# Dealing the opening loads of a transformer kernel over two DMA queues in the order of need

## The chip, the cores and the metric

The kernel runs on 1 core of one Trainium2 chip. The metric is device time in microseconds (us), lower is better. The six runs of the kernel before lie within 0.7 us of each other. "Faster" or "slower" needs 2%. Engines: TensorE (PE, with its weight loads PEld), VectorE (DVE), ScalarE (ACT), GpSimd (POOL), SyncE (SP). "SPq" and "ACTq" are DMA issues by SyncE's and ScalarE's sequencers. A load has "landed" when its semaphore tells that all its data are there.

## The reference, cut to what matters

Two rounds of a windowed attention layer and a gated MLP, on 2048 tokens of width 1024, bf16. Only the first steps of the first layer matter here: layer norm of x, then q = norm(x) times the first 1024 columns of `wqkv`.

```python
x = A_x                                                  # 1 x 2048 x 1024
x = x + _A_ref(_layernorm(x), A_wqkv, A_wo)              # qkv = norm(x) @ wqkv, attention, @ wo
x = x + _B_ref(_layernorm(x), B_w1, B_w3, B_w2)          # (silu(xn @ w1) * (xn @ w3)) @ w2
x = x + _A_ref(_layernorm(x), A_wqkv, A_wo)
x = x + _B_ref(_layernorm(x), B_w1, B_w3, B_w2)
```

## The kernel before

The kernel lists its operations with estimated durations, places them in a small model of the engines, and emits them in the order of the modelled start. Each engine then works through its own list in that fixed order. The queue "AQ" is a model: in the model it is an engine of its own, but its loads are issued by ScalarE and stand in ScalarE's list, between its activations.

```python
def dma(kb, dst, src, reads, writes, cls=3, transpose=False, queue="SP"):
    def emit(op):
        if queue == "AQ":
            nc.scalar.dma_start(dst, src)      # ScalarE's own instruction list
        ...
        else:
            nc.sync.dma_start(dst, src)
    return pr.add(queue, 0.45, emit, reads, writes, cls, size=kb * 1024)
```

PE starts with ten warm-up matmuls on a constant (line 285), while the first loads are under way. The opening works on four blocks of 128 tokens, x0 to x3, and on the q weights, cut into eight "rows" of 128 x 1024 (256 KB each). x0 comes as two halves. Blocks 0 and 1 are multiplied without waiting for their variance: half of x0's sum is formed on VectorE, the other half on ScalarE, the mean is subtracted, PE transposes the result, and the weight matmuls of blocks 0 and 1 start, row by row. Blocks 2 and 3 are normalized meanwhile and multiplied afterwards.

```python
def q_first():
    for hh in range(2):                                   # x0: one half on each queue
        dma(128, x_sb[0][:, hh * 512:(hh + 1) * 512], ..., queue="AQ" if hh else "SP")
    dma(256, x_sb[1][:], xin[:, 1, :], ..., queue="AQ")
    rows = q_weights(0, "k", load=False)
    for kk in range(4):
        rows[2](kk)                                       # rows 0 to 3, SyncE
    load_x(0, 2, 4)                                       # x2, x3, SyncE
    rows[2](4)
    rows[2](5)
    ...
    act(0.75, ... accum_out=part[:, 1:2] ...)             # ScalarE: sum of x0's second half
    rows[2](6, 2, queue="AQ", after=[("part", 1)])        # rows 6 and 7, one load, ScalarE
    ...                                                   # mean, subtract, transposes
    for j in range(2, TPC):
        stats(j)                                          # VectorE: statistics of x2, x3
        ...
    # PE (line 509): rows 0 to 2 for x0, rows 0 to 2 for x1, then rows 3 to 7 for both
    for kk, j0, j1 in [(k, j, j + 1) for j in range(2) for k in range(3)] + [(k, 0, 2) for k in range(3, KT)]:
        ...
    # PE (line 523): all rows for x2 and x3
```

Of the kernel before, what the change touches and what calls it, by code (L numbers as in the profile page):

```python
# [156 lines left out]
def kernel(  # L157
# [42 lines left out]
    def alloc(name, shape, dt=BF16):  # L200
        return sb.tile(shape, dt, name=name)
# [31 lines left out]
    part = alloc("part", [P, 2], FP32)  # L233
# [14 lines left out]
    def dve(dur, emit, reads, writes, cls=2, **kw):  # L248
        return pr.add("DVE", dur, emit, reads, writes, cls, **kw)

    def act(dur, emit, reads, writes, cls=0, **kw):
        return pr.add("ACT", dur, emit, reads, writes, cls, **kw)
# [4 lines that stand above are left out]
                nc.scalar.dma_start(dst, src)  # L257
            elif transpose:
                nc.sync.dma_start_transpose(dst, src)
# [3 lines that stand above are left out]
# [34 lines left out]
    def load_x(c, j0=0, j1=TPC, after=()):  # L297
        for j in range(j0, j1):
            n = c * TPC + j
            dma(256, x_sb[n][:], xin[:, n, :], after, [("x", n, 0), ("x", n, 1)], 0 if c == 0 else 3)  # L300
# [3 lines left out]
    def ln(c, first=False):  # L304
        s = stage_no[0]
        b, q = s % 2, s % 4
        xb = xnT[b]

        def stats(j, after=()):
            n = c * TPC + j  # L310
            pri = -9 if first else 1
            for hh in range(2):
                dve(0.67, lambda _, hh=hh: nc.vector.bn_stats(st[q][:, j, hh, :],  # L313
                                                              x_sb[n][:, hh * 512:(hh + 1) * 512]),
                    [("x", n, hh)] + list(after), [("st", q, j, hh)], pri)
            dve(0.2, lambda _: nc.vector.bn_aggr(mv[q][:, j, :], st[q][:, j, :, :]),  # L316
                [("st", q, j, 0), ("st", q, j, 1)], [("mv", q, j)], pri)

        def root(j0, j1):
            act(0.3, lambda _: nc.scalar.activation(sd[q][:, j0:j1], mv[q][:, j0:j1, 1], ACTF.Sqrt, bias=epst[:]),  # L320
                [("mv", q, j) for j in range(j0, j1)] + ["eps"], [("sd", q, j) for j in range(j0, j1)], -9 if first else 0, table="sqrt")
            dve(0.16, lambda _: nc.vector.reciprocal(rstd[q][:, j0:j1], sd[q][:, j0:j1]),
                [("sd", q, j) for j in range(j0, j1)], [("rstd", q, j) for j in range(j0, j1)], -9 if first else 0)

        def apply(j):
            n = c * TPC + j
            dve(0.5, lambda _: nc.vector.tensor_scalar(xn[j][:], x_sb[n][:], mv[q][:, j, 0:1], rstd[q][:, j:j + 1],  # L327
                                                       op0=ALU.subtract, op1=ALU.mult),
                [("x", n, 0), ("x", n, 1), ("mv", q, j), ("rstd", q, j)], [("xn", j)] + [("xn", j, h) for h in range(2)], -9 if first else 1)

        if first:
            return b, q, stats, root, apply
        for j in range(TPC):
            stats(j)
        root(0, TPC)
        for j in range(TPC):
            apply(j)
            dma(256, xb[:, :, j * P:(j + 1) * P], xn[j][:], [("xn", j)],
                [("xnT", b, j)] + [("xnT", b, j, h) for h in range(2)], 0, transpose=True)
        return b  # L340
# [17 lines left out]
    def q_weights(which, split, load=True, after=()):  # L358
        ids = [take_slot(), take_slot()]
        if not load:  # L360
            def row(kk, n=1, after=(), **kw):
                i = ids[kk // 4]
                v = slot[i][:].rearrange("p (k c) -> p k c", k=4)
                dma(256 * n, v[:, kk % 4:kk % 4 + n, :], wqkv_v[:, kk:kk + n, which * D:(which + 1) * D], after,
                    [("w", i, kk % 4 + z) for z in range(n)], 0, **kw)
            return ids, split, row
        for h, i in enumerate(ids):
            if split != "c":
                v = slot[i][:].rearrange("p (k c) -> p k c", k=4)
                dma(1024, v, wqkv_v[:, 4 * h:4 * h + 4, which * D:(which + 1) * D], after,  # L370
                    [("w", i, k) for k in range(4)], 3)
            else:
                v = slot[i][:].rearrange("p (k c) -> p k c", k=KT)
                dma(1024, v, wqkv_v[:, :, which * D + h * 512:which * D + (h + 1) * 512], [],
                    [("w", i, k) for k in range(4)], 3)
        return ids, split
# [43 lines left out]
    def transposed(src, keys, dst, dkeys):  # L420
        for h, add, fn, dur in ((0, dve, nc.vector.tensor_copy, 0.42), (1, act, nc.scalar.copy, 0.59)):
            a = Acc()
            k0 = 4 * h

            def tr(op, a=a, k0=k0):
                pt = bank[a.bank][:].bitcast(BF16)
                for k in range(4):
                    nc.tensor.transpose(pt[:, k * P:(k + 1) * P], src[:, (k0 + k) * P:(k0 + k + 1) * P], ident[:])  # L428
            tro = pr.add("PE", 0.25, tr, [keys[h], "ident"], [], takes=[a], lag=0.17, lane=2)

            def emit(op, a=a, k0=k0, fn=fn):
                pt = bank[a.bank][:].bitcast(BF16)
                fn(dst[:, k0:k0 + 4, :], pt[:, 0:4 * P].rearrange("p (k t) -> p k t", k=4))
            evac(add, dur, emit, tro, [], dkeys[k0:k0 + 4], a, cls=-9)

    def q_first():
        for hh in range(2):
            dma(128, x_sb[0][:, hh * 512:(hh + 1) * 512], xin[:, 0, hh * 512:(hh + 1) * 512], [], [("x", 0, hh)], 0,
                queue="AQ" if hh else "SP")
        dma(256, x_sb[1][:], xin[:, 1, :], [], [("x", 1, 0), ("x", 1, 1)], 0, queue="AQ")  # L440
        rows = q_weights(0, "k", load=False)
        wslots[0] = rows[:2]
        for kk in range(4):
            rows[2](kk)
        load_x(0, 2, 4)
        rows[2](4)
        rows[2](5)
        b, q, stats, root, apply = ln(0, first=True)
        ce = hT[:, 8:16, :]
        dve(0.45, lambda _: nc.vector.tensor_scalar(xn[2][:, 0:512], x_sb[0][:, 0:512], 0.0, 0.0, op0=ALU.add,  # L450
# [1 line left out]
            [("x", 0, 0)], [("xn", 2), ("part", 0)], -9)  # L452
        act(0.75, lambda _: nc.scalar.activation(xn[3][:, 0:512], x_sb[0][:, 512:1024], ACTF.Copy,
                                                 accum_out=part[:, 1:2]), [("x", 0, 1)], [("xn", 3), ("part", 1)], -9)
        rows[2](6, 2, queue="AQ", after=[("part", 1)])
        dve(0.16, lambda _: nc.vector.tensor_scalar(mean[:, 0:1], part[:, 0:1], part[:, 1:2], 1.0 / D, op0=ALU.add,
                                                    op1=ALU.mult), [("part", 0), ("part", 1)], [("mean", 0)], -9)
        act(1.15, lambda _: nc.scalar.activation(xn[3][:], x_sb[1][:], ACTF.Copy, scale=1.0 / D,
# [7 lines left out]
            transposed(xn[j], [("xn", j, h) for h in range(2)], ce[:, :, j * P:(j + 1) * P],  # L466
                       [("ce", j, k) for k in range(KT)])
        for j in range(2, TPC):
            stats(j)
            root(j, j + 1)  # L470
            apply(j)
            transposed(xn[j], [("xn", j)] * 2, xnT[b][:, :, j * P:(j + 1) * P],
                       [("xnT", b, j, k // 4) for k in range(KT)])
# [233 lines left out]
    def attend(l, c):  # L707
        for r in range(R):
            t_stage(l, c * R + r)

    q_first()
    attend(0, 0)
    for c in range(1, NCH):
# [47 lines left out]
```

## Time and profile before

| | before |
|---|---|
| median of 6 runs | 1616.09 us (1615.54 to 1616.23) |
| profiled span | 1614.2 us |
| PE busy | 1601.5 us |
| first weight matmul (line 509) | 5.89 us |
| idle of PE at row 4 | 0.91 us, from 10.25 to 11.16 |
| second half of the opening (line 523) starts | 15.56 us |

The page of the kernel before; first its busy times, then the chain that ended last, by engine.

```profile
PE 1601.5 (99%) x7463; PEld 762.6 (47%) x7610; DVE 1121.5 (69%) x1904; ACT 331.3 (21%) x527; POOL 5.2 (0%) x28
...
PE 99%; DMA 1%; issue 0%; SPq 0%; DVE 0%
```

PE is the bound nearly everywhere. The waits of PE over the whole span (who waited for what: us in total, times, longest):

```profile
PE bank L509 <- DMA slot<-in_A_wqkv_dram: 0.9, 1, 0.9
PE bank L285 <- PEq L745: 0.8, 1, 0.8
PE bank L509 <- DVE hT L433: 0.3, 1, 0.3
```

These three waits are all that the view lists, and all lie in the opening: a change of the loads can win about 0.9 us. (The trace of this kernel lacks 147 matmul records, 7463 against 7610 weight loads, so PE's busy time is understated.) The timeline of PE (start, length, what) shows where. Matmuls are pipelined, so lengths overlap a little.

```profile
4.98 0.66 PE L428 MATMUL bank<-ident,xn 128*128 128x128 bf16 x8
5.89 1.05 PE L509 MATMUL bank<-hT,slot 128*128 128x128 bf16 x16 [0.25 <-DVE hT L433]
...
7.42 2.83 PE L509 MATMUL bank<-hT,slot 128*128 128x128 bf16 x40
11.16 2.79 PE L509 MATMUL bank<-hT,slot 128*128 128x256 bf16 x24 [0.91 <-DMA slot<-in_A_wqkv_dram]
...
15.56 7.15 PE L523 MATMUL bank<-xnT,slot 128*128 128x256 bf16 x64
```

ScalarE in the same time. Its issue of rows 6 and 7 (ACTq at 3.57) stands behind the first activation on x0 (line 453).

```profile
0.80 0.88 ACTq L257 DMA_DIRECT2D x<-in_A_x_dram  x2
2.02 0.20 ACT L281 ACTIVATE preload<-const-float32-0.0 128x1 f32<-128x1 f32 x1
3.56 0.63 ACT L453 ACTIVATE xn<-x 128x512 bf16<-128x512 bf16 x1 [1.34 <-DMA x<-in_A_x_dram]
3.57 0.39 ACTq L257 DMA_DIRECT2D slot<-in_A_wqkv_dram  x1
```

### The profile page before, as it was taken

The numbers are of one execution on the slowest core, as the hardware profiler recorded it, in microseconds if no ns is written. First come the engines' busy times: TensorE is split into PE (matmuls) and PEld (weight loads), VectorE is DVE, ScalarE is ACT, GpSimd is POOL, SyncE is SP. The second block draws the span as 40 slices with busy tenths as digits, with TensorE's granted clock in tenths as the row PEclk, the third lists the DMA queues.
The fourth block names the chain that finished last, engine by engine and source line by source line (L and its number), as shares of the span: only waits on it lengthen the run. The fifth ranks groups of instructions, "written<-read, shape, count | busy, mean of one in ns | idle before, by whom it ended". The sixth has DMA issues, their size and how long they took to land.

```text
span 1614.2 us, 19079 instructions
## 1 busy us (share of the span) xinstructions
PE 1601.5 (99%) x7463; PEld 762.6 (47%) x7610; DVE 1121.5 (69%) x1904; ACT 331.3 (21%) x527; POOL 5.2 (0%) x28
## 2 busy tenths in 40 slices
PE   9999999999999999999999999999999999999999
PEld 6555544444444444444444444444444444444444
DVE  5898888889889888888898729884288832211211
ACT  5423322021211222113211032110321101101110
POOL 1000000000000000000000000000000000000000
PEclk9999999999999999999999999999999999999999
DMA  9834755395548664758645487365873464454451
GB/s 320 228 100 150 224 170 171 118 225 168 171 136 251 195 190 132 217 167 234 189 136 160 160 243 231 122 173 176 253 221 119 158 181 156 144 176 150 156 165 44
DMA packets 350777, 285.80 MB, mean 177 GB/s; under 512 B 72288, under 2 KB 344928, under 8 KB 350688
## 3 DMA queue, kind: packets, MB, share of 16 engines
q1 hardware_dynamic: 350128, 283.67, 58.2%
q8 instruction: 59, 0.97, 0.2%
q10 hardware_dynamic: 560, 0.92, 0.2%
q14 instruction: 30, 0.25, 0.0%
HBM read 238.94 MB, written 29.36 MB: 166 GB/s over the span
## 4 chain that ended last, share of the span: by engine, by line
PE 99%; DMA 1%; issue 0%; SPq 0%; DVE 0%
PE bank L347 98%; DMA slot<-in_A_wqkv_dram 1%; PE bank L523 0%; PE bank L509 0%; PE bank L428 0%; SPq L261 0%; DVE x L688 0%
## 5 line engine op out<-in xcount | busy, mean ns | idle before, releaser
L347 PE MATMUL bank<-xnT,slot 128*128 128x512 bf16 x4955 | 1088.9, 379 | 5.3
L347 PEld LDWEIGHTS <-slot 128*128 128x128 bf16 x5056 | 518.1, 102 | 573.0
L347 PE MATMUL bank<-slot,hT 128*128 128x512 bf16 (+2 forms) x1812 | 387.3, 372 | 1.9
L658 DVE TENSOR_TENSOR hT<-sg,bank 128x512 bf16<-128x512 bf16 x224 | 153.4, 685 | 213.0 <-PE bank L347 196.3
L265 DVE TENSOR_TENSOR scr<-scr 128x1024 bf16<-128x1024 bf16 (+3 forms) x576 | 292.1, 535 | 2.1
L347 PEld LDWEIGHTS <-hT 128*128 128x128 bf16 x1848 | 178.5, 98 | 208.7
L656 ACT ACTIVATE sg<-bank 128x512 bf16<-128x512 f32 x224 | 133.8, 597 | 653.8 <-PE bank L347 613.6
L265 DVE TENSOR_TENSOR scr<-qT,kT 128x2048 bf16<-128x2048 bf16 x128 | 153.7, 1216 | 71.7 <-DMA kT<-qkv_d 70.1
L405 ACT CAST sgt<-bank 128x512 bf16<-128x512 f32 x184 | 107.9, 586 | 290.9 <-PE bank L347 273.1
L265 DVE TENSOR_TENSOR scr<-pA,vT 128x2048 bf16<-128x2048 bf16 x128 | 152.5, 1216 | 0.4
L688 DVE TENSOR_TENSOR x<-x,bank 128x512 bf16<-128x512 bf16 (+1 forms) x66 | 43.7, 669 | 122.7 <-PE bank L347 122.4
L347 PE MATMUL bank<-wo,oT 128*128 128x512 bf16 x502 | 112.6, 379 | 0.5
L313 DVE BATCH_NORM_STATS2 st<-x 128x6 f32<-128x512 bf16 x124 | 81.5, 679 | 11.5 <-DMA x<-in_A_x_dram 11.0
L347 PEld LDWEIGHTS <-oT 128*128 128x128 bf16 x512 | 50.1, 98 | 60.3
L633 DVE TENSOR_TENSOR x<-x,bank 128x512 bf16<-128x512 bf16 x64 | 43.9, 685 | 36.5 <-PE bank L347 35.0
L320 ACT ACTIVATE sd<-mv,epst 128x4 f32<-128x4 f32 (+1 forms) x17 | 5.1, 299 | 182.4 <-DVE mv L316 181.9
L616 DVE STREAM_TRANSPOSE pA<-pB 128x2048 bf16<-128x2048 bf16 x16 | 37.0, 2310 | 0.4
L593 DVE STREAM_TRANSPOSE pB<-pA 128x2048 bf16<-128x2048 bf16 x16 | 37.0, 2310 | 0.4
L656 ACT ACT_TABLE_LOAD x20 | 25.7, 1283 | 51.3 <-PE bank L347 51.1
L265 DVE TENSOR_TENSOR pA<-scr 128x256 bf16<-128x256 bf16 x128 | 35.3, 282 | 0.3
L327 DVE TENSOR_SCALAR xn<-x,mv,rstd 128x1024 bf16<-128x1024 bf16 x62 | 30.8, 541 | 4.6 <-DMA xnT<-xn 4.5
L265 DVE TENSOR_TENSOR oT<-scr 128x256 bf16<-128x256 bf16 x128 | 33.6, 282 | 0.1
(60 smaller groups left out, 210.0 us busy)
## 6 DMA issues: line engine op xcount, KB each, us to landing
slot<-in_B_w_dram SPq DMA_DIRECT2D x160, 1024.0 KB, 5.8
slot<-in_A_wqkv_dram SPq DMA_DIRECT2D x28, 1024.0 KB, 5.2
qkv_d<-sgt SPq DMA_DIRECT2D x92, 256.0 KB, 3.4
qT<-qkv_d SPq DMA_DIRECT2D x16, 512.0 KB, 5.0
slot<-in_B_w_dram SPq DMA_DIRECT2D x16, 512.0 KB, 5.5
kT<-qkv_d SPq DMA_DIRECT2D x14, 544.0 KB, 6.6
vT<-qkv_d SPq DMA_DIRECT2D x14, 544.0 KB, 5.7
out_dram<-x SPq DMA_DIRECT2D x31, 128.0 KB, 4.2
```

Source lines behind the costliest of these rows:

```text
L265: return lambda _: nc.vector.tensor_tensor(o, a, b, op=op)
L313: dve(0.67, lambda _, hh=hh: nc.vector.bn_stats(st[q][:, j, hh, :], x_sb[n][:, hh * 512:(hh + 1) * 512]), [("x", n, hh)] + list(after), [( ...
L320: act(0.3, lambda _: nc.scalar.activation(sd[q][:, j0:j1], mv[q][:, j0:j1, 1], ACTF.Sqrt, bias=epst[:]), [("mv", q, j) for j in range(j0, ...
L327: dve(0.5, lambda _: nc.vector.tensor_scalar(xn[j][:], x_sb[n][:], mv[q][:, j, 0:1], rstd[q][:, j:j + 1], op0=ALU.subtract, op1=ALU.mult), ...
L347: nc.tensor.matmul(bank[a.bank][:, 0:ncol], lhsT=w, rhs=r, start=first and i == 0, stop=last and i == n - 1)
L405: evac(act, 0.59, lambda _, a=a, i=i, m=m: nc.scalar.copy(sgt[i][:, m % 2, :], bank[a.bank][:]), op, [], [("sgt", i, m % 2)], a)
L593: dve(2.31, lambda _: nc.vector.transpose(psmT[:].rearrange("p c d -> p (c d)"), psm[:].rearrange("p w s -> p (w s)")), allA, ["pB"])
L616: dve(2.31, lambda _: nc.vector.transpose(At[:].rearrange("p w s -> p (w s)"), AeT[:].rearrange("p c d -> p (c d)")), ["pB"], allA)
L633: evac(dve, t1(512), lambda _, xs=xs, a=a: nc.vector.tensor_tensor(xs, xs, bank[a.bank][:], op=ALU.add), op, [("x", n, hh)], [("x", n, hh) ...
L656: evac(act, 0.6, lambda _, i=i, a=ag: nc.scalar.activation(sg[i][:], bank[a.bank][:], ACTF.Silu), og, [], [("sg", i)], ag, table="silu")
L658: evac(dve, t1(512), lambda _, i=i, a=au, f=f: nc.vector.tensor_tensor(hT[:, f, :], sg[i][:], bank[a.bank][:], op=ALU.mult), ou, [("sg", i ...
L688: evac(dve, t1(cn), lambda _, xs=xs, a=a, cn=cn: nc.vector.tensor_tensor(xs, xs, bank[a.bank][:, 0:cn], op=ALU.add), op, [("x", n, hh)], [ ...
```

## The change: its intent, and the diff

The intent is to give each row of weights a place in the order of need, by dealing the loads over both queues. Rows 2, 3 and 4 move to ScalarE's queue; x2 and x3 go ahead of rows 5 to 7 on SyncE's. Since x2 can now come early, its statistics are held until the copy of x1's transpose, so that they don't get in VectorE's way.

```diff
-        for kk in range(4):
+        for kk in range(2):
             rows[2](kk)
+        for kk in range(2, 5):
+            rows[2](kk, queue="AQ")
         load_x(0, 2, 4)
-        rows[2](4)
         rows[2](5)
+        rows[2](6, 2)
 ...
-        rows[2](6, 2, queue="AQ", after=[("part", 1)])
 ...
         for j in range(2, TPC):
-            stats(j)
+            stats(j, [("ce", 1, 0)])
```

## The prediction

> **What bounds the kernel.** TensorE (PE). The page gives PE 1601.5 us of a 1614.2 us span, and the chain that ended last is 99% PE, 1% DMA. The waits of PE from 25 us to the end list nothing. The change touches only the first 15 us, so its ceiling is PE's idle time there. The timeline of PE shows it: nothing before 0.77 (launch), 0.25 us before the first weight matmuls at 5.89 (a VectorE copy), and 0.91 us from 10.25 to 11.16, put down to a load of the q weights. That last gap is what can be won: 0.06% of the time.
>
> **Why the gap is there.** By the trace SyncE issues x0's half, weight rows 0 to 3, then x2 (3.08), x3 (4.98), row 4 (5.71), row 5 (6.08). x3 and row 4 are held until rows 0 and 1 have landed (4.97, 5.70): loads reuse a few completion semaphores, and the ninth and later wait for an early one. ScalarE's queue brings x0's other half, x1 (landed 5.15), and at 3.57 rows 6 and 7. Those land at 9.74, before row 4 (11.12) and row 5 (11.79): the wrong order. PE has used up row 3 at 10.25.
>
> **What the change does.** It adds no bytes and no instruction; rows 2, 3, 4 move to ScalarE's queue, x2, x3 go ahead of rows 5, 6, 7 on SyncE's, and the statistics of x2, x3 wait for the copy of x1's transpose. The Trainium skill, "DMA: Bandwidth & Descriptors" (Issuing engines are not separate DMA queues), says that both queues run on the same 16 DMA engines and that only issue time is saved. The trace agrees: by the view by windows the DMA share is about 1.0, at 380 to 406 GB/s, from 4 to 15 us. So the last of the 3.1 MB still lands near 11.7 us, but now it is rows 6 and 7. Estimates at that rate: rows 1, 2 land near 6.4 (row 1 was 5.70), row 3 and x2 near 7.7, row 4 and x3 near 9, row 5 near 10.4. PE needs row 4 at 10.25, row 5 at 11.1, rows 6, 7 at 12.0 (0.87 us a row): the gap closes, just.
>
> **What it costs.** ScalarE issues five loads (0.44 us each) before its first real activation: 0.80 to about 3.0, hidden by the wait for x0 (activation at 3.56). Unless the fifth, row 4, has to wait for a semaphore: for x0's half (3.29) it would cost 0.2 us; for row 0 (4.97) ScalarE's mean of x0 would start near 5.4, PE's first weight matmul near 7.7, and more would be lost (about 0.5 us net) than won. I give that 35%. Row 1's later landing may cost PE 0.1 us.
>
> **Sum.** Good case -0.8 us, bad case +0.3 to +0.6, weighted about -0.4; everything behind 16 us is PE-bound and moves along. Predicted 1615.5 us, range 1614.6 to 1616.8; chances 0.005 faster, 0.99 same, 0.005 slower.
>
> **What would show it right.** The timeline of PE: no gap at row 4; second-half matmuls (L523 before) start near 14.7, not 15.56. Landings in the order of need, the last near 11.7. ScalarE's first activation on x0 near 3.56. Wrong: ScalarE's issue of row 4 begins after 3.3 and PE's first weight matmul after 6.2; or a new PE wait for rows 6 and 7 or xn3's transposes; or PE idle elsewhere.
>
> **What would make it wrong.** The semaphore wait above; a misplaced transpose in PE's fixed order; a reshuffled schedule later; chip-to-chip differences as large as the effect.

## The result, and the profile after

| | before | after |
|---|---|---|
| median of 6 runs | 1616.09 us | 1619.91 us (1619.22 to 1621.62) |
| ratio after / before, 95% interval | | 1.0026 [1.0013, 1.0039] |
| ScalarE's first activation on x0 | 3.56 us | 7.64 us |
| first weight matmul | 5.89 us | 9.97 us |
| second half of the opening starts | 15.56 us | 19.67 us |

A ratio is the mean time of one kernel's fast runs over that of the other's of the same rounds, so it is not quite the ratio of the medians. The changed kernel is 3.8 us slower. It is "the same" at the limit of 2%, but its six runs and those of before lie far apart.

PE's own list of instructions is the same in both kernels, apart from line numbers (509 became 510, 523 became 524, 453 became 455). So the time can be followed along one list. PE of the changed kernel:

```profile
9.06 0.87 PE L428 MATMUL bank<-ident,xn 128*128 128x128 bf16 x8 [3.86 <-DVE xn L464]
9.97 1.87 PE L510 MATMUL bank<-hT,slot 128*128 128x128 bf16 x16
...
12.48 5.58 PE L510 MATMUL bank<-hT,slot 128*128 128x128 bf16 x64
...
19.67 7.15 PE L524 MATMUL bank<-xnT,slot 128*128 128x256 bf16 x64
```

The gap at row 4 is gone, as was intended. In its place there is a gap of 3.86 us before the very first transpose, and it was VectorE's subtraction of the mean that ended it. VectorE in turn waited for ScalarE:

```profile
8.40 0.21 DVE L457 TENSOR_SCALAR mean<-part 128x1 f32<-128x1 f32 x1 [4.40 <-ACT xn L455]
8.65 0.62 DVE L464 TENSOR_SCALAR xn<-x,mean 128x512 bf16<-128x512 bf16 x2
```

ScalarE of the changed kernel:

```profile
1.68 0.45 ACTq L257 DMA_DIRECT2D slot<-in_A_wqkv_dram  x1
2.02 0.20 ACT L281 ACTIVATE preload<-const-float32-0.0 128x1 f32<-128x1 f32 x1
3.30 4.29 ACTq L257 DMA_DIRECT2D slot<-in_A_wqkv_dram  x2
7.64 0.63 ACT L455 ACTIVATE xn<-x 128x512 bf16<-128x512 bf16 x1 [5.42 <-DMA slot<-in_A_wqkv_dram]
```

The third line is the cause. It merges ScalarE's issues of rows 3 and 4 from 3.30 to 7.59 us. The issue records in the trace give the detail, as read in the next table: row 3's issue starts at 3.30, as soon as x0's first half has landed (3.28), and row 4's at 7.26, as soon as row 1 has landed (7.24). Only then does ScalarE come to its activation on x0, whose data had been there since 3.50. The merged line alone would look like two slow issues; the wait in brackets on the activation names the weights, not x.

One view misleads here. The chain that ended last puts the start of the first weight matmul (9.97) down to a load, row 5, which landed at 9.95. Row 5 is not needed yet; it only shares row 0's semaphore. VectorE's copy of x0's transpose ended at 9.92, and the matmul began 0.05 us later, just as in the kernel before (5.84 and 5.89).

The trace has, for each load, the issue, the semaphore that tells of its landing, and the wait before the issue. Eight semaphores, numbered 103 to 110, are used in turn, over both queues together; the ninth and later load waits until the earlier load with the same semaphore has landed. By these numbers row 4, though only the fifth load on ScalarE's queue, is the eleventh of the program, so it waits for the third, row 1. It did so in the kernel before as well (issue at 5.71, row 1 landed at 5.70), but there SyncE issued it, and no computation stood behind it. Times in us from the start of the span (the recorded texts differ from them by 0.01 here and there):

| load | before: queue, issue, landing | after: queue, issue, landing | after: issue waits for |
|---|---|---|---|
| x0, halves | SP 0.74, 3.28; ACT 0.80, 3.54 | SP 0.74, 3.28; ACT 0.79, 3.50 | |
| x1 | ACT 1.22, 5.15 | ACT 1.20, 5.00 | |
| row 0 | SP 1.19, 4.96 | SP 1.19, 4.76 | |
| row 1 | SP 1.66, 5.70 | SP 1.66, **7.24** | |
| row 2 | SP 2.13, 6.53 | ACT 1.68, 7.95 | |
| row 3 | SP 2.60, 7.71 | ACT 3.30, 9.45 | x0, first half |
| row 4 | SP 5.71, 11.11 | ACT **7.26**, 13.48 | **row 1** |
| x2 | SP 3.08, 8.65 | SP 2.13, 8.13 | |
| x3 | SP 4.98, 10.44 | SP 2.60, 8.64 | |
| row 5 | SP 6.08, 11.79 | SP 4.78, 9.95 | row 0 |
| rows 6, 7 | ACT 3.57, 9.74 | SP 5.15, 11.29 | x0, second half |

The Trainium skill, "DMA: Bandwidth & Descriptors" (Anatomy of one DMA, a section on GpSimd's path), says of semaphore waits in general that they happen on the issuing sequencer before dispatch. The trace agrees for ScalarE's queue: the wait is at ScalarE, 3.6 us from 3.64 (end of row 3's issue) to 7.26, with no activation in between.

A second thing changed. The view by windows (window and its length, busy us and count for PE, PEld, DVE, ACT and POOL, then PEclk, which is the granted share of PE's full clock, DMA share, GB/s), first of the kernel before, then of the changed one:

```profile
9.00:10.00 1.00, 1.00 (x15) 0.90 (x12) 0.96 (x2) 1.00 (x3) 0.00 (x0) 1.00 1.04 389
10.00:11.00 1.00, 0.25 (x3) 0.00 (x0) 0.54 (x1) 0.48 (x2) 0.00 (x0) 1.00 1.06 401
```

```profile
9.00:10.00 1.00, 0.90 (x9) 0.70 (x10) 0.77 (x4) 0.58 (x3) 0.00 (x0) 0.67 1.00 358
10.00:11.00 1.00, 1.00 (x11) 1.00 (x11) 0.31 (x1) 0.55 (x1) 0.00 (x0) 0.50 1.02 391
11.00:12.00 1.00, 1.00 (x12) 1.00 (x11) 0.00 (x0) 0.00 (x0) 0.00 (x0) 0.50 1.05 381
12.00:13.00 1.00, 1.00 (x14) 1.00 (x12) 0.70 (x2) 0.27 (x1) 0.00 (x0) 0.62 1.05 406
```

PEclk falls to 0.50 just after PE comes back to work, and the same 16 matmuls take 1.87 us instead of 1.05. The trace's clock records put the half clock at 9.34 to 12.75 us.

The sum up to the second half: the first weight matmul is 4.08 us later (9.97 - 5.89). From there to the second half it took 9.67 us before (15.56 - 5.89), of which 0.91 us was the gap, and takes 9.70 us now without the gap. So the gap's 0.91 us was won, and as much, 0.94 us (9.70 - 9.67 + 0.91), was lost again on the way. (The slower matmuls alone cost more: the same way without a gap and at full clock takes 8.39 us in two experiments below, 1.31 less than 9.70. Some smaller stalls, 0.37 us, went with the gap.) The second half starts 4.11 us later in all; at the end of the span 3.9 us are left (1618.1 - 1614.2), and the medians differ by 3.82.

### The profile page after: what moved, and what is told of

Its sections match the earlier page's. It is cut to its first block, busy times and chain, and to the rows that moved or that the text cites. A ratio compares the mean times of both kernels' runs of the same rounds, so it can differ in the third digit from the quotient of the medians.

```text
span 1618.1 us, 19226 instructions
## 1 busy us (share of the span) xinstructions
PE 1610.8 (100%) x7610; PEld 764.2 (47%) x7610; DVE 1122.0 (69%) x1904; ACT 331.0 (20%) x527; POOL 5.2 (0%) x28
## 4 chain that ended last, share of the span: by engine, by line
PE 99%; DMA 1%; SPq 0%; DVE 0%; issue 0%
PE bank L347 98%; DMA slot<-in_A_wqkv_dram 1%; PE bank L510 1%; PE bank L524 0%; PE bank L428 0%; SPq L261 0%; DVE x L689 0%
```

## The experiments

Theory A: the loss comes from where row 4's issue stands. It waits for row 1, in ScalarE's list, ahead of ScalarE's half of the mean of x0, on which PE's whole start depends. Theory B: two queues that share the DMA engines bring the needed rows later, and PE is late for that reason. Two more suspects: the hold of the statistics, and PE's clock. In all but one variant (the one without the hold) PE's order in the opening is that of the kernel before and the changed one, apart from added warm-ups; only in the last variant does it differ later on, where, by the order of the weight loads, a group of 8 moves behind the 32 that followed it. Two sets of four ran, each on one chip with its runs of the kernel before (median 1616.08 and 1616.00 us). The changed kernel was not timed again beside them, so its 1619.91 us is compared across rounds. All outputs are right.

### Row 3 back to SyncE: row 4's issue waits for x0 instead of row 1

Edit, against the changed kernel:

```diff
-        for kk in range(2, 5):
-            rows[2](kk, queue="AQ")
+        rows[2](2, queue="AQ")
+        rows[2](3)
+        rows[2](4, queue="AQ")
```

> Row 3 goes back to SyncE, row 4 stays on ScalarE's queue as its fourth load, so that its issue waits for the semaphore of x0's half instead of row 1's; PE's order of work is the changed kernel's. Theory A (the changed kernel loses because ScalarE's fifth issue, held until row 1 has landed at 7.24 us, stands in ScalarE's program before its mean of x0): the issue of row 4 starts near 3.3 us, ScalarE's first activation on x0 near 3.75 (7.64 in the changed kernel), PE's first weight matmul near 6.0 to 6.2 (9.97), PE clock never halved, time 1615.3 to 1616.3 us. Theory B (two queues that share the DMA engines make rows 0 to 2 land late, and PE waits for the loads): rows still share, PE starts late, time above 1618 us.

Measured: 1615.66 us (1615.26 to 1616.08), ratio 0.9998 [0.9986, 1.0011]. Row 4's issue and the activation, then PE:

```profile
3.40 0.34 ACTq L257 DMA_DIRECT2D slot<-in_A_wqkv_dram  x1
3.78 0.63 ACT L456 ACTIVATE xn<-x 128x512 bf16<-128x512 bf16 x1 [1.56 <-DMA x<-in_A_x_dram]
```

```profile
6.11 0.61 PE L511 MATMUL bank<-hT,slot 128*128 128x128 bf16 x8 [0.25 <-DVE hT L433]
7.29 0.62 PE L511 MATMUL bank<-hT,slot 128*128 128x128 bf16 x8 [0.58 <-DMA slot<-in_A_wqkv_dram]
```

The whole loss is gone, with row 4 still on ScalarE's queue and still ahead of the mean. So neither the queue nor four issues that don't wait long cost anything to speak of; the wait for row 1 does. Theory B is right in a small part: row 1 landed at 7.25 us here too (5.70 before), and PE waits 0.58 us for it.

### Rows 2 and 3 as one load: row 4's issue waits for row 0

```diff
-        for kk in range(2, 5):
-            rows[2](kk, queue="AQ")
+        rows[2](2, 2, queue="AQ")
+        rows[2](4, queue="AQ")
```

> A dose of the wait: rows 2 and 3 are one load of 512 KB on ScalarE's queue, everything else as in the changed kernel; same bytes on the same queues in the same order, but one load fewer, so row 4's issue waits for row 0 (landed 4.76 us in the changed kernel) instead of row 1 (7.24). Theory A: issue of row 4 ends near 5.1, first activation on x0 near 5.2, PE's first weight matmul near 7.5, time 1616.5 to 1617.7 us depending on whether PE's clock drops in the shorter idle stretch. Theory B: the same traffic gives the same time as the changed kernel, 1619.9 us.

Measured: 1617.81 us (1616.30 to 1618.14), ratio 1.0010 [0.9997, 1.0022]. Row 0 landed at 5.16 us in this profile, and ScalarE followed it:

```profile
5.18 0.34 ACTq L257 DMA_DIRECT2D slot<-in_A_wqkv_dram  x1
5.57 0.63 ACT L455 ACTIVATE xn<-x 128x512 bf16<-128x512 bf16 x1 [3.35 <-DMA slot<-in_A_wqkv_dram]
```

PE's first weight matmul is at 7.90 us. This is a dose of the wait between the two others: activation at 3.78, 5.57, 7.64 us gives first weight matmuls at 6.11, 7.90, 9.97, each 2.33 us after the activation, and medians of 1615.66, 1617.81, 1619.91. The bytes, queues and their order are those of the changed kernel (though row 5's issue on SyncE moved from 4.78 to 3.36 us, since its semaphore changed too), and all five runs lie between the two others' (1616.30 to 1618.14), so theory B's number (1619.9) is excluded. The median is 0.1 us above the stated range; PE's clock did halve in the profile (7.75 to 11.16 us), which the range had left open. The record has a mean granted clock for each run: the four at 0.999 took 1617.66 to 1618.14 us, the one at 1.000 took 1616.30.

### More warm-up matmuls in the changed kernel

The tenth of PE's warm-up operations emits 18 matmuls instead of one:

```diff
-        pr.add("PE", 0.43, lambda op: nc.tensor.matmul(... rhs=one, start=True, stop=True), takes=[a])
+        pr.add("PE", 0.43, lambda op, n=1 if i < NWARM - 1 else 18: [
+            nc.tensor.matmul(... rhs=one, start=True, stop=True) for _ in range(n)], takes=[a])
```

> The changed kernel with 17 more warm-up matmuls after the ten, which keep PE busy until about 8.9 us; nothing else moves. If the halved PE clock after 9 us (0.5 to 0.67 granted from 9 to 13 us) comes from PE's 3.9 us of idleness, the granted clock stays 1.0, the first 16 weight matmuls take about 1.05 us again (1.87), and the time falls by 1.0 to 1.5 us to 1618.4 to 1618.9; PE's first weight matmul stays near 9.8. If the clock drop has nothing to do with idleness: 1619.9 us and the clock still halved.

Measured: 1618.66 us (1617.98 to 1618.95), ratio 1.0015 [1.0001, 1.0029]. PE and the clock:

```profile
0.77 8.54 PE L286 MATMUL bank<-const-bfloat16-1.0 128*128 128x512 bf16 x27 [0.77 <-PEq L747]
...
10.04 1.05 PE L511 MATMUL bank<-hT,slot 128*128 128x128 bf16 x16 [0.29 <-DMA slot<-in_A_wqkv_dram]
```

```profile
10.00:11.00 1.00, 0.96 (x18) 0.95 (x18) 0.39 (x1) 0.38 (x1) 0.00 (x0) 1.00 1.03 399
```

The first weight matmul is as late as in the changed kernel, but the clock stays at 1.00 (in all five runs the mean is 1.000), and the way from there to the second half takes 8.39 us (18.43 - 10.04) instead of 9.70. The halved clock comes from PE's idleness and is worth 1.25 us of the 3.8 (1619.91 - 1618.66), by medians of different rounds; the timeline's 9.70 - 8.39 gives 1.31. (The bracket on the first weight matmul names a load, but as above it follows VectorE's copy, 9.57 to 9.99. In this profile row 1 landed at 6.64 and ScalarE came to x0 at 7.04, so it was the added matmuls themselves, over only near 9 us, that kept the first weight matmul at 10.04. The figure is that exact and no more.) The remaining 2.6 us is the late start (4.15 us, 10.04 - 5.89) less the 1.28 us by which the way to the second half is now shorter than before (9.67 - 8.39, of which the gap was 0.91): 2.87 us there, 2.7 at the end of the span.

### Only row 4 back to SyncE

```diff
-        for kk in range(2, 5):
+        for kk in range(2, 4):
             rows[2](kk, queue="AQ")
         load_x(0, 2, 4)
+        rows[2](4)
         rows[2](5)
```

> Only row 4 goes back to SyncE's queue, between x3 and row 5; rows 2 and 3 stay on ScalarE's. ScalarE's last issue before its mean of x0 then waits only for x0's half. Theory A: first activation on x0 near 3.75 us, PE's first weight matmul near 6.1, no gap of PE at row 4 if it lands before 10.2, time 1615.2 to 1616.2 us. Theory B (sharing itself): rows 0 to 3 are shared between the queues as in the changed kernel, so most of its loss stays, above 1618 us.

Measured: 1615.18 us (1614.87 to 1615.99), ratio 0.9996 [0.9983, 1.0008]; activation on x0 at 3.86 us, first weight matmul at 6.23, and no gap at row 4.

```profile
3.86 0.63 ACT L456 ACTIVATE xn<-x 128x512 bf16<-128x512 bf16 x1 [1.63 <-DMA x<-in_A_x_dram]
```

Row 4's issue, now SyncE's, still waited for row 1 (it starts at 7.08) and cost nothing there. Taking one load out of ScalarE's list takes away the whole loss, and the median falls 0.9 us below that of before (the runs overlap, and the interval contains 1). Row 1 is late here as well (7.06 us), with a PE wait of 0.28 us.

### Row 4's load placed behind ScalarE's means

```diff
-        for kk in range(2, 5):
+        for kk in range(2, 4):
             rows[2](kk, queue="AQ")
 ...
             [("xn", 3), ("mean", 1)], -9)
+        rows[2](4, queue="AQ", after=[("mean", 1)])
```

> The changed kernel with row 4's load at the same queue and on the same semaphore, but placed in ScalarE's program behind its means of x0 and x1. Theory A (what costs is the place of the held issue before the mean of x0): first activation on x0 near 3.8 us and PE's first weight matmul near 6.2 as with row 4 on SyncE, no halved clock at that point. But the issue then starts at 6.2 to 7.2 and the load, behind rows 5 to 7 and the k weights, lands only near 12.5 to 13.5, so PE gets a new gap of 2 to 3 us at row 4: 1617.2 to 1618.5 us. Theory B (sharing itself): PE's first weight matmul stays near 10 and 1619.9 us.

Measured: 1615.60 us (1615.05 to 1615.79), ratio 0.9997 [0.9984, 1.0009].

```profile
3.67 0.63 ACT L455 ACTIVATE xn<-x 128x512 bf16<-128x512 bf16 x1 [1.44 <-DMA x<-in_A_x_dram]
...
5.12 0.33 ACTq L257 DMA_DIRECT2D slot<-in_A_wqkv_dram  x1
```

ScalarE's and PE's starts came out as theory A said (3.67 and 6.21 us), but the rest of the expectation missed. In this order row 4 did not share row 1's semaphore; it took x1's, for whose landing ScalarE had just waited anyway, so the issue went out at 5.12 us, and the row landed at 11.09. The expected gap of 2 to 3 us at row 4 did not come; PE waited 0.5 us for loads in all, at earlier rows. The statement "on the same semaphore" in the expectation was wrong: moving a load in one list renumbered the semaphores of those that follow.

### The changed kernel without the hold of the statistics

```diff
-            stats(j, [("ce", 1, 0)])
+            stats(j)
```

> The changed kernel without the hold of the statistics of x2 and x3. Theory A: the hold has nothing to do with the loss; first activation on x0 stays near 7.6 us, PE's first weight matmul near 10, 1619.3 to 1620.5 us. Rival (the hold delays the normalized x2, x3 and with them PE): the time falls back by 1 us or more.

Measured: 1620.06 us (1619.76 to 1621.19), ratio 1.0028 [1.0014, 1.0041]. The hold is not the cause of the loss. One number missed in the profile: the activation came at 6.36 us, because row 1 happened to land at 5.95 in this execution, and the first weight matmul at 8.90. Yet the second half started at 19.52 us, no earlier to speak of than with 9.97 (19.67), since the half clock lasted from 6.80 to 13.63 us here. A slightly earlier start was eaten up by a longer slow stretch. PE's order differs in this variant (the transposes of x2 and x3 stand two rows earlier), so it tells less than the others.

### The kernel before with the hold added

```diff
-            stats(j)
+            stats(j, [("ce", 1, 0)])
```

> The kernel before with only the hold added; PE's order is the same. x2 landed at 8.65 us there, after the copy that the hold waits for (7.82), so the hold does nothing: 1615.7 to 1616.4 us. Rival: up to 1 us slower.

Measured: 1615.74 us (1615.54 to 1616.25), ratio 0.9999 [0.9987, 1.0012]. The hold by itself does nothing that the runs show, and the gap at row 4 is still there:

```profile
11.12 2.79 PE L509 MATMUL bank<-hT,slot 128*128 128x256 bf16 x24 [0.89 <-DMA slot<-in_A_wqkv_dram]
```

### The kernel before with rows 4 and 6, 7 exchanged

This takes from the change only the order of the weights. Against the kernel before:

```diff
         load_x(0, 2, 4)
-        rows[2](4)
         rows[2](5)
+        rows[2](6, 2)
 ...
-        rows[2](6, 2, queue="AQ", after=[("part", 1)])
+        rows[2](4, queue="AQ", after=[("part", 1)])
```

> Out of what the first four runs showed: the kernel before with only the weights' order mended. The first eight loads stay as they were (rows 0 to 3 on SyncE alone, so row 1 should land near 5.7 us and not near 7.1 as where the queues share); row 4 takes the place of rows 6 and 7 on ScalarE's queue behind the mean of x0 (issue near 3.6), and rows 6 and 7 go last on SyncE. PE's first weight matmul near 5.9, row 4 landed by 9.5, no gap of PE at row 4 (0.91 us before), the second half's matmuls start near 14.7 (15.56 before): 1615.0 to 1615.5 us, no more than row 4 on SyncE (1615.18) and perhaps less. If the gap only moves to rows 5 to 7 or to the transposes of x3, 1615.8 to 1616.3.

Measured: 1614.96 us (1614.86 to 1615.10), ratio 0.9994 [0.9981, 1.0006]. PE:

```profile
6.14 1.05 PE L509 MATMUL bank<-hT,slot 128*128 128x128 bf16 x16
...
7.47 5.45 PE L509 MATMUL bank<-hT,slot 128*128 128x128 bf16 x64
...
14.53 7.15 PE L523 MATMUL bank<-xnT,slot 128*128 128x256 bf16 x64
```

No gap is left: the view of waits lists only PE's wait for the launch. The second half starts 1.03 us earlier than before (15.56 - 14.53), and the medians differ by 1.04 us. Row 1 landed at 5.84, row 4 at 9.02, and rows 6 and 7 last, at 11.72. This is the fastest kernel. Its five runs and the nine of the kernel before beside it (1615.72 to 1616.22) don't overlap, though the stated interval of the ratio, wider than these spreads, contains 1.

## Why the prediction was wrong, point by point

- "What bounds the kernel" and "Why the gap is there" were right. The gap at row 4 was worth what the prediction said: closing it without a new wait gave 1.04 us in the last experiment (0.91 us of gap and some smaller stalls).
- "The gap closes" was right for the changed kernel only by luck: row 4 landed at 13.48 us, not near 9, and so later than in the kernel before, but PE came to it later still. "Landings in the order of need" failed with it: row 4 came last of the q weights.
- The step that failed is in "What it costs": the fifth issue on ScalarE's queue. The prediction named the mechanism, a held issue ahead of ScalarE's mean of x0, but gave it a chance of only 35% and took row 0 (4.97 us) as the worst load to wait for. It was row 1, landed at 7.24 us: row 4 is not the ninth or tenth load, to which x0's half and row 0 fall, but the eleventh. How the loads would be numbered in the changed kernel was not in the profile of before; that eight semaphores are used in turn was, and the prediction itself reads there that row 4 was held until row 1 had landed.
- "Estimates at that rate: rows 1, 2 land near 6.4" was mis-sized. With rows shared over the queues row 1 landed at 7.24 us in the changed kernel, at 5.95 to 7.25 in the six experiments that share them, and at 5.70 before. As row 4's issue waited for just this load, the error went straight into the time: with row 1 at 6.4 ScalarE's mean would have started near 6.8 (estimated from the 0.40 us between landing and mean in the changed kernel); it started at 7.64. (The rate was also read a little high: in windows of 1 us it is 361 to 402 GB/s in the kernel before, not 380 to 406.)
- "About 0.5 us net" for the bad case missed a whole term: PE idles 3.9 us, its clock halves for 3.4 us, and that costs 1.25 us more by the warm-up experiment. The bad case as predicted, a wait for row 0, was run as "rows 2 and 3 as one load": mean and first weight matmul came at 5.57 and 7.90 us (predicted 5.4 and 7.7), so the path was right; but the median was 1.73 us above the kernel before (1617.81 - 1616.08), and only 0.22 in the one run at full clock.
- So the sum "-0.4" became +3.8. The range of 1614.6 to 1616.8 held the bad case as it was sized (+0.3 to +0.6), but not the one that came, a wait for row 1 with a halved clock, to which the text gave no chance.
- "Everything behind 16 us is PE-bound and moves along" was right: 4.11 us at the start of the second half, 3.9 us at the end.

What stays open: why row 1 lands up to 1.5 us later in kernels where the other queue has more loads in flight (the profiles go together so, but no run shows the cause), and why its landing varies so (5.95 to 7.24 us between profiles with the same first eight loads). By the table x1 and row 0, the pair before, landed no later than before. The trace shows where the delay sits: each load has sixteen semaphore updates, and in the changed kernel fourteen of row 1's had come by 5.99 us; the last two came at 6.69 and 7.24. In the kernel before all sixteen came from 5.18 to 5.70. The six timed runs of the changed kernel spread over 2.4 us. The clock has a part in this: the four with a mean granted clock of 0.999 took 1619.22 to 1619.92 us, the two with 0.998 took 1620.57 and 1621.62. (A stretch of 3.41 us at half clock takes 0.001 off the mean over 1618 us.) Whether row 1's landing made the difference between them cannot be seen, since one run alone was profiled.

## What to carry to other kernels

A load issued from ScalarE stood in its list like any other instruction: while its semaphore was taken by a load in flight, everything behind it waited (3.64 to 7.26 us). Before loads are moved to such a queue, count the loads of all queues together against the number of semaphores in turn (eight here), look up which landing the late ones wait for, and put those behind the engine's critical work or on the engine that only issues (on SyncE the same wait, to 7.08 us, cost nothing that shows). When PE is kept waiting at the start, add the cost of a slower clock to the wait itself (1.25 us here).

## What the Trainium skill lacked or had wrong

- "DMA: Bandwidth & Descriptors", Issuing engines are not separate DMA queues: it says that issuing on several engines only saves sequencer time. The total rate agrees (some 340 to 410 GB/s in both kernels from 4 to 15 us). What it lacks is the price on an engine that also computes: a held issue stopped ScalarE from 3.64 to 7.26 us and cost 3.8 us in all. It says that loads interleave, but not how late a single one can become by it: row 1 landed at 5.95 to 7.25 us in seven profiles with rows on two queues from the start, at 5.70 to 6.28 us in three with rows 0 to 3 on one. The ranges overlap, and the cause is not shown.
- "TensorE: Matmul & The Clock Gate", Part 1: The HAM clock gate, gives a window of 3413 ns that runs freely, and a drop to half the clock after at least one idle window. The step agrees: the half clock lasted 3.41 us in two kernels (9.34 to 12.75, and 7.75 to 11.16) and twice that in a third (6.80 to 13.63). Fully idle a window need not be: counted in windows of 3.41 us from the first clock record of each trace, the clock also fell after one in which PE was busy for 1.16 us (0.66 of them transposes; the longest idle stretch was 2.15 us; rows 2 and 3 as one load), and it stayed full after one with 2.11 us busy, again 0.66 of them transposes (row 3 on SyncE). No run shows whether transposes count.
- The same page has no figure for how busy a window must be to bring the full clock back: 2.35 of 3.41 us at half clock did not (the variant without the hold; 1.04 of them transposes), 3.26 and 3.37 us did.
